# Two value blocks ahead of a weight on the queue, their shifted copies by DMA, and an attention pair moved earlier: a fused attention and MLP kernel

## The chip, the cores and the metric

The kernel runs on one core of a Trainium2 chip. The metric is the device time of one launch in microseconds (us), the median of several runs. The engines are TensorE (PE; its weight loads are shown as PEld), VectorE (DVE), ScalarE (ACT), GpSimd (POOL) and SyncE (SP). POOL and SP also issue most DMA transfers: SP's go through queue 1, ACT's through queue 10, POOL's through queue 0, and all of them run on the same 16 DMA engines.

## The reference

Attention with a sliding window of 32 positions to each side feeds a two-layer MLP with ELU:

```python
# q, k, v: (8 batches, 8 heads, 576 positions, 64), float32
scores = q @ k.T / 8
scores = where(abs(i - j) <= 32, scores, -1e9)
attn = softmax(scores)
x = (attn @ v) laid out as (4608 tokens, 512)
h = x @ w_in                               # w_in (512, 2048)
g = where(h > 0, h, exp(min(h, 0)) - 1)
out = g @ w_out                            # w_out (2048, 512), float32
```

## The kernel before

**Attention.** A batch has 9 query blocks of 64; two successive blocks make a pair, so there are 36 pairs, and pair i covers blocks 2i and 2i+1 for all heads. For a pair TensorE computes the scores (L296), ScalarE the exponential (`exponential`, L307), VectorE multiplies by a mask (`mask`, L316), TensorE multiplies by the values (`pv`, L328; a column of ones beside each head's values gives the sum), and VectorE divides (`normalize`, L337 and L340). The result is transposed, on TensorE for the first ten pairs (`x_transpose`, L349, with a copy by `x_evac`), and by a DMA after that, and lands in `xT`, the left operand of the MLP.

**Values.** A query block needs 128 values that begin 32 positions ahead of it. `V_e` holds five blocks m = 0 to 4 of 128 positions (`load_v(b, m)`, a cast from float32 to bfloat16 on POOL's queue), which serve the even query blocks. `V_o` holds the same values shifted by 64 positions, for the odd query blocks; it is made from `V_e` by moving partitions 64 to 127 to 0 to 63 and back (`rotate_v`, VectorE copies, L152). Pair 2 (query blocks 4 and 5) needs `V_e` block 2 and `V_o` block 2; pair 3 (blocks 6 and 7) needs blocks 3 of both. `V_o` block 2 is made of values 2 and 3, block 3 of values 3 and 4.

**Queries and keys.** They come in float32 by `load_qk` and are cast by `cast_qk` on ScalarE or VectorE, or come through `load_cast`, which casts on the way in on POOL's queue. TensorE transposes them (`transpose_qk`; L271 from the cast buffer, two narrow transposes for each one at L266 from `load_cast`'s). Batches 0 and 1 come in two halves, `HALF_A` and `HALF_B`.

**MLP.** 4608 tokens make 18 tiles of 256. A step is one tile and one eighth of d_ff: `mm1` (L582, 8 matmuls into `ps`), the exponential (L589), the subtraction of 1 (L591) and the max/min that makes `g_sb` (`elu`, L601), and later `mm2` (L616, 4 matmuls into `psY`). The order of the first 16 steps is: tile 0's first four, tile 1's first four, then both in turn. The weights come in quarters on POOL's queue, each serving two steps of a tile: w_in(0) and w_out(0) serve steps 0, 1, 4 and 5, w_in(1) and w_out(1) steps 2, 3, 6 and 7, quarters 2 and 3 steps 8 to 11 and 12 to 15.

**What sets the order.** It is written out by hand. The front part of the program has batch 0's first half of q and k, pairs 0 and 1 and the second half. Then a loop over steps kk runs, in this order, `elu(kk - 1)`, the tasks in slot "dve", `mm1(kk)`, the tasks in slot "mid", the second products due (`mm2`), and slot "end". `at(kk, slot, fn, ...)` puts a task there. Each engine works through its own instructions in program order, so a task that waits holds back all that stands behind it on the same engine.

The second products normally lag by two steps; for the first steps a table gives them:

```python
for n in {1: (0,), 2: (), 3: (), 4: (), 5: (2,), 6: (3, 4)}.get(
        kk, (kk - LAG,) if kk >= LAG else ()):
    mm2(n)
```

and `mm2(1)` is a task of step 2. POOL's queue is served in order. Before, after batch 0's second half of q and k, it holds w_in(0), w_out(0), values 3 and 4 of batch 0, w_in(1), w_out(1), w_in(2), w_out(2), values 0 to 2 of batch 1, w_in(3), w_out(3), values 3 and 4 of batch 1. SyncE's transfers of batch 1's and 2's q and k are held back by `gate`, a transfer of one element that reads a weight and so waits until it has landed (the first on w_out(0), the second on w_in(3)).

Of the kernel before, what the change touches and what calls it, by code (L numbers as in the profile page):

```python
# [10 lines left out]
BF16 = mybir.dt.bfloat16  # L11
# [10 lines left out]
def kernel(  # L22
# [9 lines left out]
    nc = tc.nc  # L32

    B, H, S, D = q.shape
# [3 lines left out]
    D_MODEL = H * D  # L38
# [7 lines left out]
    SJ = S // NC  # L46
    VS = 5
# [5 lines left out]
    NFO = D_FF // 128  # L53
# [7 lines left out]
    cpool = ctx.enter_context(tc.tile_pool(name="const", bufs=1))  # L61
# [32 lines left out]
    def ps_tile(shape, dt, tag, name):  # L94
# [7 lines left out]
          for i in range(2)]  # L102
    V_e = [cpool.tile([128, VS, H, VD], BF16, name=f"Ve{i}") for i in range(3)]
    V_o = [cpool.tile([128, VS - 1, H, VD], BF16, name=f"Vo{i}")
           for i in range(3)]
    w_in_sb = wpool.tile([128, NDO, D_FF], BF16, name="w_in_sb")
    w_out_sb = wpool.tile([128, NFO, D_MODEL], BF16, name="w_out_sb")
# [4 lines left out]
    WHOLE, HALF_A, HALF_B = (0, SJ), (0, SJ // 2), (1, SJ // 2)  # L112
    qk_f = {}

    def load_qk(b, which, part, engs=(nc.sync, nc.sync)):
        z, nj = part
        t = lpool.tile([128, 2, nj * D], FP32, tag=f"f{which}{nj}",
                       name=f"f{which}")
        qk_f[b, which, z] = t
        src = (q, k)[which][b, :, z * NC * nj:(z + 1) * NC * nj, :].rearrange(  # L120
            "(g h) (c j) d -> c g h (j d)", h=2, j=nj)
        for h in range(2):
            engs[h].dma_start(out=t[:, h, :], in_=src[:, :, h, :])
# [3 lines left out]

    def load_cast(b, which, part):
        z, nj = part
        t = cpool.tile([128, 2, nj * D], BF16, name=f"c{which}")  # L130
        qk_c[b, which, z] = t
        src = (q, k)[which][b, :, z * NC * nj:(z + 1) * NC * nj, :].rearrange(
            "(g h) (c j) d -> c g h (j d)", h=2, j=nj)
        for h in range(2):
            nc.gpsimd.dma_start(out=t[:, h, :], in_=src[:, :, h, :])  # L135

    def load_v(b, m):
        lo = 128 * m - WIN
        p0 = max(0, -lo)
        p1 = min(128, S - lo)  # L140
        nc.gpsimd.dma_start(  # L141
            out=V_e[b % 3][p0:p1, m, :, 0:D],
            in_=v[b, :, lo + p0:lo + p1, :].rearrange("h p d -> p h d"))
# [5 lines left out]
    def rotate_v(b, m0, m1, parts=(0, 1)):  # L149
        e, o = V_e[b % 3], V_o[b % 3]  # L150
        for z in parts:
            nc.vector.tensor_copy(o[64 * z:64 * (z + 1), m0:m1],  # L152
                                  e[64 * (1 - z):64 * (2 - z),
                                    m0 + z:m1 + z])

# [2 lines left out]
    def gate(src, dt=BF16, eng=nc.sync):  # L160
        gates[0] += 1
        t = cpool.tile([1, 1], dt, name=f"gate{gates[0]}")
        eng.dma_start(out=t, in_=src)

    def load_w_in(c):
        w = D_FF // 4
        nc.gpsimd.dma_start(
            out=w_in_sb[:, :, c * w:(c + 1) * w],
            in_=moe_w_in[:, c * w:(c + 1) * w].rearrange(
                "(o p) f -> p o f", p=128))  # L170

    def load_w_out(c):
        n = NFO // 4
        nc.gpsimd.dma_start(
            out=w_out_sb[:, c * n:(c + 1) * n, :],
            in_=moe_w_out[c * n * 128:(c + 1) * n * 128, :].rearrange(
                "(o p) f -> p o f", p=128))

    def w_in_at(c):
        return w_in_sb[0:1, 0, (c + 1) * (D_FF // 4) - 1:(c + 1) * (D_FF // 4)]  # L180
# [7 lines left out]
    def edges(i):  # L188
# [19 lines left out]
        out=masks, in_=masks, compare_op=ALU.is_ge, fill=0.0,  # L208
        base=0, pattern=[[0, 5], [-1, QB]], channel_multiplier=1)
    nc.gpsimd.affine_select(  # L210
        out=masks, in_=masks, compare_op=ALU.is_ge, fill=0.0,
# [183 lines left out]
    for which in range(2):  # L395
        load_cast(0, which, HALF_B)
    load_w_in(0)
    for mi in (0, 4):
        nc.gpsimd.affine_select(
            out=masks[:, mi, :], in_=masks[:, mi, :], compare_op=ALU.is_ge,  # L400
            fill=0.0, base=-WIN, pattern=[[0, QB]], channel_multiplier=1)
    nc.gpsimd.affine_select(
        out=masks[:, 3, :], in_=masks[:, 3, :], compare_op=ALU.is_ge,
        fill=0.0, base=128 - WIN - 1, pattern=[[0, QB]],
        channel_multiplier=-1)
    load_w_out(0)
    for m in (3, 4):
        load_v(0, m)
    for c in (1, 2):
        load_w_in(c)  # L410
        load_w_out(c)
    for m in range(3):
        load_v(1, m)
    load_w_in(3)
    load_w_out(3)
    for m in range(3, VS):
        load_v(1, m)
    gate(w_out_sb[0:1, NFO // 4 - 1, D_MODEL - 1:D_MODEL])
    for which in range(2):
        load_qk(1, which, HALF_A)  # L420
    gate(w_in_at(3))
    for which in range(2):
        load_qk(1, which, HALF_B)
    for which in range(2):
        load_qk(2, which, WHOLE)

    idle(8, "y1")
    front_cast(0, HALF_A, nc.vector)
# [6 lines left out]
    for i, tag in ((0, "s"), (1, "u")):  # L435
        scores(i, tag)
        exponential(i)
    idle(4, "y0")
    rotate_v(0, 0, 2)
    for i in (0, 1):  # L440
        mask(i)
# [10 lines left out]
    idle(2, "h1")  # L452

    tasks = {}

    def at(kk, slot, fn, *args):
        tasks.setdefault((kk, slot), []).append((fn, args))  # L460

    def run(kk, slot):
        for fn, args in tasks.get((kk, slot), ()):
            fn(*args)
# [8 lines left out]


    at(0, "mid", scores, 2, "s")
    at(0, "mid", exponential, 2)
    at(0, "mid", scores, 3, "u")
    at(1, "mid", exponential, 3)
    at(1, "dve", mask, 2)
    at(2, "dve", lambda: mm2(1))  # L480
    at(2, "dve", rotate_v, 0, 2, VS - 1)
    at(2, "dve", mask, 3)
    for i in (2, 3):
        at(2, "dve", pv, i)
        at(2, "dve", normalize, i)
        at(3, "mid" if i == 3 else "dve", x_transpose, i)
        at(3, "mid" if i == 3 else "dve", x_evac, i, nc.scalar)
    at(4, "dve", swap_pools)

    for part, kq in ((HALF_A, 7), (HALF_B, 15)):  # L490
        for which in range(2):
            at(*((kq + which, "dve") if kq == 7 else (kq - 1 + which, "mid")),
               cast_qk, 1, which, part, 0, SJ // 2,
               (nc.scalar, nc.vector)[which])
            at(kq + which, "mid", transpose_qk, 1, which, part, 0, SJ // 2,
               nc.scalar, "s")
    at(6, "dve", edges, 2)
    at(16, "dve", hold_v, 2)
    for m in range(VS):
        at(16 + m, "mid", load_v, 2, m)  # L500
    at(12, "dve", rotate_v, 1, 0, 2)
    for z in range(2):
        at(14 + z, "dve", rotate_v, 1, 2, VS - 1, (z,))
# [7 lines left out]
    for i in range(4, NPAIR):  # L511
        two = i >= FIRST_TWO
        kk, z = begin[i], i % 2 if two else 0
# [5 lines left out]
        n = kk + (3 + z if two else 2)  # L519
# [9 lines left out]
    for b in range(2, B):  # L529
# [9 lines left out]
        for n, back in enumerate((3, 2, 1, 0) if b == 2 else (10, 8, 3, 2)):  # L539
            m0 = 2 * (n // 2)  # L540
# [55 lines left out]
    def elu(kk, z=0):  # L596
        if z == 0:
            g_t[kk] = mpool.tile([128, FG, TT], BF16, tag="g_sb", name="g_sb")
        ps = psH[kk][z]
        w = ps.shape[1]  # L600
        nc.vector.scalar_tensor_tensor(  # L601
            g_t[kk][:, z * w:(z + 1) * w, :], ps, 0.0, m_t[kk][z],
            ALU.max, ALU.min)
# [3 lines left out]
    def mm2(kk):  # L607
        t, s = order[kk]
        if s == 0:
            psY[t] = [ps_tile([128, D_MODEL], FP32, g, "psY")  # L610
                      for g in (("h2", "t0") if t == 1 else ("y0", "y1"))]
        g_sb = g_t.pop(kk)
        last = t == NT - 1 and s == STEPS - 1
        for ts in range(2):
            for j in range(FG):
                nc.tensor.matmul(  # L616
                    psY[t][ts],
                    lhsT=g_sb[:, j, ts * 128:(ts + 1) * 128],
                    rhs=w_out_sb[:, s * FG + j, :],
                    start=(s == 0 and j == 0),  # L620
                    stop=(s == STEPS - 1 and j == FG - 1))
        if s == STEPS - 1:
            for ts in range(2):
                z = 1 - ts if last else ts
                eng = (nc.scalar, nc.vector)[z]
                y_sb = opool.tile([128, D_MODEL], FP32, tag=f"y_sb{z}",
                                  name="y_sb")
                copy_on(eng, y_sb, psY[t][ts])
                (nc.scalar if last and ts else nc.sync).dma_start(
                    out_t[t, :, ts, :], y_sb)  # L630

    LAG = 2
    for kk in range(NSTEP + LAG):
        run(kk, "first")
        if 1 <= kk < NSTEP:
            elu(kk - 1)
        run(kk, "dve")
        if kk < NSTEP:
            mm1(kk)
        run(kk, "mid")  # L640

        for n in {1: (0,), 2: (), 3: (), 4: (), 5: (2,), 6: (3, 4)}.get(
                kk, (kk - LAG,) if kk >= LAG else ()):
            mm2(n)
        run(kk, "end")
# [30 lines left out]
```

The softmax here doesn't subtract the row's maximum and nothing guards it: scores larger than these inputs give would overflow.

## Time and profile before

| | before |
|---|---|
| time, median of 3 runs | 311.01 us (310.62 to 311.11) |
| span of the profiled execution | 307.9 us |
| TensorE busy | 291.5 us (95%) |
| VectorE busy | 245.8 us (80%) |
| ScalarE busy | 169.4 us (55%) |
| POOL's queue 0 | 42304 packets, 9.51 MB |
| SyncE's queue 1 | 47444 packets, 35.60 MB |
| w_in from issue to landing, median of 4 | 14.0 us |
| w_out from issue to landing, median of 4 | 16.6 us |
| batch 1's halves of q and k from issue to landing, within the first 100 us | 5.4 and 7.2 us |

Times in the profile are counted from the first instruction. A line of a timeline gives start and length, the engine, the source line, what it writes and reads, how many instructions were merged, and in brackets how long the engine had been idle and who ended that. The landing of a DMA is when its last part has signalled. TensorE's busy time counts overlapping stages of its pipeline, so single groups look longer than the distance from one to the next (a first product takes 1.04 us by itself and 0.87 us in a row).

### The profile page before, as it was taken

To read this page: it belongs to the slowest core of one execution; us is meant where nothing else is said; L and a number is where in the kernel's file an instruction comes from. 1 tells how busy PE (TensorE), PEld (TensorE's weight loads), DVE (VectorE), ACT (ScalarE), POOL (GpSimd) and SP (SyncE) were. 2 spreads that over 40 slices of the span, in tenths; PEclk is the share of its full clock that TensorE was granted. 3 is DMA by queue.
4 is the path that set the end of the run, shared out by engine and by line. 5 is a ranking of instruction groups with operands and counts; after the bars stand their busy time and mean duration, and the time that the engine had idled before them with its cause. 6 is when DMAs were issued, how large, how long until landed. Compare 5 with 4: busy or idle time off the path is not lost.

```text
span 307.9 us, 7525 instructions
## 1 busy us (share of the span) xinstructions
PE 291.5 (95%) x3009; PEld 196.9 (64%) x3062; DVE 245.8 (80%) x478; ACT 169.4 (55%) x254; POOL 45.8 (15%) x64
## 2 busy tenths in 40 slices
PE   6778999999999999999999999999999999999994
PEld 2546666676666666666666666666666666666662
DVE  6776688899978788888887888888888787876663
ACT  3635656787664674767376737673636363634331
POOL 8841100952220302020202010000000000000000
PEclk9799999999999999999999999999999999999999
DMA  9999999999999899799999998377111111111011
GB/s 188 190 193 273 188 257 387 302 191 223 293 166 195 289 255 206 170 165 331 156 140 197 322 261 183 111 178 159 70 36 68 36 70 35 70 34 70 0 70 68
DMA packets 91654, 52.33 MB, mean 170 GB/s; under 512 B 76516, under 2 KB 81124, under 8 KB 91620
## 3 DMA queue, kind: packets, MB, share of 16 engines
q1 hardware_dynamic: 47444, 35.60, 47.4%
q0 software_dynamic: 42304, 9.51, 40.1%
q10 hardware_dynamic: 1872, 6.75, 5.8%
q8 instruction: 24, 0.39, 0.5%
q14 instruction: 10, 0.08, 0.1%
HBM read 36.70 MB, written 15.34 MB: 169 GB/s over the span
## 4 chain that ended last, share of the span: by engine, by line
PE 81%; DVE 7%; DMA 4%; POOL 3%; issue 2%; ACT 1%; DVEq 0%; POOLq 0%
PE ps L582 38%; PE psY L616 36%; DMA w_in_sb<-in_moe_w_in_dram 4%; PE psS L328 3%; PE psS L296 3%; DVE g_sb L601 2%; POOL Ve L141 1%; PE ptx L271 1%; DVE m_sb L591 1%; DVE x_st L340 1%; DVE pm L316 1%; ACT e_sb L589 1%; POOL c L135 1%; DVE y_sb L228 1%; PE psXT L349 1%
## 5 line engine op out<-in xcount | busy, mean ns | idle before, releaser
L589 ACT ACTIVATE e_sb<-ps 128x512 f32<-128x512 f32 (+1 forms) x145 | 86.2, 595 | 123.0 <-PE ps L582 115.4
L582 PE MATMUL ps<-xT,w_in_sb 128*128 128x256 bf16 x1152 | 149.3, 273 | 2.7 <-DVE m_sb L591 0.9
L616 PE MATMUL psY<-w_out_sb,g_sb 128*128 128x512 bf16 x525 | 139.1, 379 | 4.2 <-DMA w_out_sb<-in_moe_w_out_dram 0.9
L582 PEld LDWEIGHTS <-w_in_sb 128*128 128x128 bf16 x1152 | 110.7, 98 | 41.0 <-issue 2.3
L601 DVE SCALAR_TENSOR_TENSOR g_sb<-ps,m_sb 128x512 bf16<-128x512 f32 (+1 forms) x145 | 99.5, 686 | 13.1 <-PE ps L582 0.5
L591 DVE TENSOR_SCALAR m_sb<-e_sb 128x512 bf16<-128x512 f32 (+1 forms) x145 | 62.2, 429 | 35.3 <-ACT e_sb L589 33.3
L616 PEld LDWEIGHTS <-g_sb 128*128 128x128 bf16 x576 | 54.5, 98 | 39.9 <-DVE g_sb L601 1.6
L141 POOL DMA_DIRECT2D Ve<-in_v_dram x40 | 35.0, 885 | 130.7 <-PE psS L328 93.6
L307 ACT ACTIVATE pu<-psS 128x1024 bf16<-128x1024 f32 x36 | 36.6, 1019 | 1.9 <-PE psS L296 1.9
L340 DVE TENSOR_TENSOR x_st<-psS,rc 128x512 bf16<-128x512 f32 x36 | 24.9, 692 | 2.3 <-DMA xT<-x_st 1.1
L316 DVE TENSOR_TENSOR pm<-pu,masks 128x1024 bf16<-128x1024 bf16 x36 | 24.6, 683 | 1.4 <-ACT pu L307 1.3
L226 ACT CAST qkb<-f 128x768 bf16<-128x768 f32 (+1 forms) x30 | 25.4, 848 | 0.0
L328 PEld LDWEIGHTS <-pm 128*64 128x64 bf16 x576 | 11.2, 110 | 9.7 <-DVE pm L316 6.7
L152 DVE COPY Vo<-Ve 64x1040 bf16<-64x1040 bf16 x32 | 13.8, 431 | 1.4 <-DMA Ve<-in_v_dram 0.4
L328 PE MATMUL psS<-Ve,pm 128*64 128x65 bf16 x320 | 13.8, 196 | 0.5 <-DVE pm L316 0.3
L296 PEld LDWEIGHTS <-kT 64*128 64x128 bf16 x576 | 10.0, 97 | 5.3 <-issue 4.2
L228 DVE COPY y_sb<-psY 128x512 f32<-128x512 f32 x18 | 12.3, 686 | 1.0 <-PE psY L616 0.9
L296 PE MATMUL psS<-qT,kT 64*128 64x64 bf16 x576 | 12.4, 193 | 0.5 <-DVE kT L228 0.5
L328 PE MATMUL psS<-Vo,pm 128*64 128x65 bf16 x256 | 12.4, 196 | 0.2 <-DVE pm L316 0.2
L226 ACT COPY y_sb<-psY 128x512 f32<-128x512 f32 x18 | 10.5, 583 | 2.2 <-PE psY L616 2.2
L226 ACT COPY qT<-ptx 128x1152 bf16<-128x1152 bf16 (+2 forms) x8 | 7.5, 971 | 3.1 <-PE ptx L271 2.4
L271 PE MATMUL ptx<-ident,qkb 128*128 128x128 bf16 x90 | 7.1, 223 | 2.0 <-DVE qkb L228 1.9
(35 smaller groups left out, 68.3 us busy)
## 6 DMA issues: line engine op xcount, KB each, us to landing
out_dram<-y_sb SPq DMA_DIRECT2D x35, 256.0 KB, 2.8
f<-in_q_dram SPq DMA_DIRECT2D x12, 576.0 KB, 8.4
f<-in_k_dram SPq DMA_DIRECT2D x12, 576.0 KB, 9.2
in_dram<-qkb ACTq DMA_DIRECT2D x10, 576.0 KB, 7.3
Ve<-in_v_dram POOLq DMA_DIRECT2D x24, 128.0 KB, 10.3
w_in_sb<-in_moe_w_in_dram POOLq DMA_DIRECT2D x4, 512.0 KB, 14.0
w_out_sb<-in_moe_w_out_dram POOLq DMA_DIRECT2D x4, 512.0 KB, 16.6
Ve<-in_v_dram POOLq DMA_DIRECT2D x16, 96.0 KB, 9.5
```

The costliest lines, as they stand in the source:

```text
L141: nc.gpsimd.dma_start(out=V_e[b % 3][p0:p1, m, :, 0:D], in_=v[b, :, lo + p0:lo + p1, :].rearrange("h p d -> p h d"))
L226: nc.scalar.copy(d_, s_)
L296: nc.tensor.matmul(psS[:, h % 2, hp * 128 + z * QB:hp * 128 + (z + 1) * QB], lhsT=kT[b % 2][base:base + 64, KPAD + hp * S + QB * qb - WIN: ...
L307: nc.scalar.activation(pu, _bap(psS, [psS.ap[0], [1, 1024]]), AX.Exp, scale=SCALE)
L316: nc.vector.tensor_mul(pm, pu, _bap(mm, [mm.ap[0], [0, H], [1, 2 * QB]]))
L328: nc.tensor.matmul(psS[QB * z:QB * (z + 1), par, hp * VD:(hp + 1) * VD], lhsT=pm[:, par * HP + hp, z * QB:(z + 1) * QB], rhs=vv[:, qb // 2 ...
L340: nc.vector.tensor_mul(x_st, _bap(psS, [psS.ap[0], [VD, HP], [512, 2], [1, D]]), _bap(rc, [rc.ap[0], [2, HP], [1, 2], [0, D]]))
L582: nc.tensor.matmul(ps[:, j, :], lhsT=w_in_sb[:, do, fo * 128:(fo + 1) * 128], rhs=xT[t][:, :, do, :], start=(do == 0), stop=(do == NDO - 1))
L589: nc.scalar.activation(e_sb, ps, AX.Exp)
L591: nc.vector.tensor_scalar(m_sb, e_sb, -1.0, None, ALU.add)
L601: nc.vector.scalar_tensor_tensor(g_t[kk][:, z * w:(z + 1) * w, :], ps, 0.0, m_t[kk][z], ALU.max, ALU.min)
L616: nc.tensor.matmul(psY[t][ts], lhsT=g_sb[:, j, ts * 128:(ts + 1) * 128], rhs=w_out_sb[:, s * FG + j, :], start=(s == 0 and j == 0), stop=( ...
```

## The change

Values 3 and 4 of batch 0 go ahead of w_out(0) on POOL's queue. The shifted copies of them that `rotate_v` made on VectorE in step 2 are made by two SyncE transfers from SBUF to SBUF instead (`rotate_v_dma`). Batch 1's first half of q and k, which came in float32 through SyncE behind the first gate and was cast on ScalarE and VectorE in steps 7 and 8, comes through `load_cast` on POOL's queue, into the buffers that batch 0's second half used (the tag gives both the same buffer); the first gate goes. Pair 2's and pair 3's work stands sooner: both exponentials in step 0, both masks and both `pv` in step 1, pair 2's `normalize` and transpose in step 1, pair 3's in step 2. The second products 2 to 4 stand at steps 4 to 6, as in the rest of the program, rather than at steps 5 and 6. The purpose is to have the attention of pairs 2 and 3 out of the way before the second quarter of the weights is there, and the engines free of the casts.

```diff
     def load_cast(b, which, part):
-        t = cpool.tile([128, 2, nj * D], BF16, name=f"c{which}")
+        t = cpool.tile([128, 2, nj * D], BF16, tag=f"c{which}",
+                       name=f"c{which}")
...
+    def rotate_v_dma(b, m0, m1):
+        e, o = V_e[b % 3], V_o[b % 3]
+        for z in range(2):
+            nc.sync.dma_start(out=o[64 * z:64 * (z + 1), m0:m1],
+                              in_=e[64 * (1 - z):64 * (2 - z), m0 + z:m1 + z])
...
-    load_w_out(0)
     for m in (3, 4):
         load_v(0, m)
-    for c in (1, 2):
-        load_w_in(c)
-        load_w_out(c)
-    for m in range(3):
-        load_v(1, m)
-    load_w_in(3)
-    load_w_out(3)
-    for m in range(3, VS):
-        load_v(1, m)
-    gate(w_out_sb[0:1, NFO // 4 - 1, D_MODEL - 1:D_MODEL])
-    for which in range(2):
-        load_qk(1, which, HALF_A)
-    gate(w_in_at(3))
-    for which in range(2):
-        load_qk(1, which, HALF_B)
-    for which in range(2):
-        load_qk(2, which, WHOLE)
+    load_w_out(0)
+    load_w_in(1)
+    load_w_out(1)
...
+    for which in range(2):
+        load_cast(1, which, HALF_A)
+    load_w_in(2)
+    load_w_out(2)
+    for m in range(3):
+        load_v(1, m)
+    load_w_in(3)
+    load_w_out(3)
+    for m in range(3, VS):
+        load_v(1, m)
+    rotate_v_dma(0, 2, VS - 1)
+    gate(w_in_at(3))
+    for which in range(2):
+        load_qk(1, which, HALF_B)
+    for which in range(2):
+        load_qk(2, which, WHOLE)
...
     at(0, "mid", scores, 2, "s")
-    at(0, "mid", exponential, 2)
     at(0, "mid", scores, 3, "u")
-    at(1, "mid", exponential, 3)
-    at(1, "dve", mask, 2)
+    for i in (2, 3):
+        at(0, "mid", exponential, i)
+        at(1, "dve", mask, i)
+        at(1, "mid", pv, i)
+    at(1, "mid", normalize, 2)
+    at(1, "end", x_transpose, 2)
+    at(1, "end", x_evac, 2, nc.scalar)
     at(2, "dve", lambda: mm2(1))
-    at(2, "dve", rotate_v, 0, 2, VS - 1)
-    at(2, "dve", mask, 3)
-    for i in (2, 3):
-        at(2, "dve", pv, i)
-        at(2, "dve", normalize, i)
-        at(3, "mid" if i == 3 else "dve", x_transpose, i)
-        at(3, "mid" if i == 3 else "dve", x_evac, i, nc.scalar)
+    at(2, "dve", normalize, 3)
+    at(2, "mid", x_transpose, 3)
+    at(2, "mid", x_evac, 3, nc.scalar)
...
-            at(*((kq + which, "dve") if kq == 7 else (kq - 1 + which, "mid")),
-               cast_qk, 1, which, part, 0, SJ // 2,
-               (nc.scalar, nc.vector)[which])
+            if part is HALF_B:
+                at(kq - 1 + which, "mid", cast_qk, 1, which, part, 0, SJ // 2,
+                   (nc.scalar, nc.vector)[which])
...
-        for n in {1: (0,), 2: (), 3: (), 4: (), 5: (2,), 6: (3, 4)}.get(
+        for n in {1: (0,), 2: (), 3: ()}.get(
                 kk, (kk - LAG,) if kk >= LAG else ()):
```

## The prediction

> **What bounds the kernel now.** I read the page first, then the chain of waits in its early part, then TensorE's timeline there, then the transfers one by one.
>
> The page says that TensorE carries the kernel:
>
> ```profile
> span 307.9 us, 7525 instructions
> ...
> PE 291.5 (95%) x3009; PEld 196.9 (64%) x3062; DVE 245.8 (80%) x478; ACT 169.4 (55%) x254; POOL 45.8 (15%) x64
> ...
> PE 81%; DVE 7%; DMA 4%; POOL 3%; issue 2%; ACT 1%; DVEq 0%; POOLq 0%
> ```
>
> 81% of the chain is TensorE. The change touches only the first 40 us, so its worth is the time that TensorE loses there. The chain over those microseconds has one large piece that isn't compute:
>
> ```profile
> 11.50 11.10 DMA w_in_sb<-in_moe_w_in_dram
> 22.59 0.05 issue
> 22.64 1.06 PE ps L582 x8
> ```
>
> The second quarter of w_in, issued by POOL at 11.50, lands at 22.59, and step 2's first product starts 0.05 us later. TensorE's timeline around it (start, duration, what, and in brackets the idle time before and who ended it):
>
> ```profile
> 15.27 1.03 PE L582 MATMUL ps<-xT,w_in_sb 128*128 128x256 bf16 x8 [0.46 <-ACT xT L226]
> ...
> 16.80 1.05 PE L582 MATMUL ps<-xT,w_in_sb 128*128 128x256 bf16 x8
> 18.72 1.02 PE L616 MATMUL psY<-w_out_sb,g_sb 128*128 128x512 bf16 x3 [0.87 <-DMA w_out_sb<-in_moe_w_out_dram]
> 19.98 1.04 PE L616 MATMUL psY<-w_out_sb,g_sb 128*128 128x512 bf16 x4 [0.24 <-DVE g_sb L601]
> ...
> 22.64 1.05 PE L582 MATMUL ps<-xT,w_in_sb 128*128 128x256 bf16 x8 [0.36 <-DMA w_in_sb<-in_moe_w_in_dram]
> ...
> 25.95 1.91 PE L582 MATMUL ps<-xT,w_in_sb 128*128 128x256 bf16 x16 [0.94 <-DVE m_sb L591]
> ...
> 28.96 1.03 PE L582 MATMUL ps<-xT,w_in_sb 128*128 128x256 bf16 x8 [0.25 <-DVE g_sb L601]
> ...
> 36.62 1.04 PE L582 MATMUL ps<-xT,w_in_sb 128*128 128x256 bf16 x8
> ```
>
> Steps 0, 1, 2, 4, 6 and 9 of the MLP start there. The reader should see that the wait for w_in at 22.64 is filled: w_out and pairs 2 and 3 are done in it, and only 0.36 us is idle just before. From 15.27 to 36.62 TensorE has 21.35 us for 9 first products (0.87 each), 7 second products (0.86 each) and about 3 us of attention: 17 us of work, so about 4.4 us of gaps. From 36.62 to 60 the stage view has 22.64 busy of 23.38: what is won or lost before step 9 is carried to the end.
>
> SyncE's timeline, and the DMA view from there to the first packets, show how a SyncE transfer fares beside a full POOL queue:
>
> ```profile
> 18.69 0.76 SPq L163 DMA_DIRECT2D gate<-w_out_sb  x1
> 19.51 1.22 SPq L123 DMA_DIRECT2D f<-in_q_dram  x2
> ```
>
> ```profile
> q0 software_dynamic: 1037, 0.96, 126.2%
> q1 hardware_dynamic: 2, 0.00, 0.1%
> ```
>
> The last two lines (queue, packets, MB, share) are of the window 18.69 to 23.37. In these 4.7 us queue 1 (SyncE) moved two tiny packets, those of the gate, while POOL's queue moved 1037. The first q load, issued at 19.51, moved nothing until 23.37 and landed 5.8 us after issue; the second, issued at 20.12, took 7.9.
>
> [...] The trace agrees that the queues share (after 23.37 they move 184 and 194 packets in 2 us), but shows a long delay before a newcomer's turn: up to 22.70 queue 1 moved nothing and queue 0 896 packets, 56 per engine. [...] the window 4.10 to 7.52 had TensorE busy 1.86 us and the next ran at clock 0.50; the window 17.76 to 21.17 had 2.25 us busy and the clock stayed.
>
> **The change, part by part.**
>
> *Order on POOL's queue.* The queue is served in order, and V3 and V4 move from behind w_out(0) to behind w_in(0). POOL can issue all of them by 13 us as before. w_in(0) landed at 15.06; V3 came 1.47 after its predecessor (18.68 to 20.15) and V4 0.36 later. So V3 lands near 16.5 and V4 near 16.9 instead of 20.15 and 20.51; w_out(0), taking 3.6, near 20.5 instead of 18.68; w_in(1) has the same bytes ahead of it as before and lands at 22.6, plus up to 0.6 for the copies below. The wait that bounded the stage isn't shortened.
>
> *The shifted copies.* Two VectorE copies of 0.44 us (0.88 at 20.17) go. Two SyncE transfers of 64 rows by 2,080 bytes (133 KB) take their place, issued when V3 and V4 have landed, about 16.5 and 17.1 (an issue takes 0.6). No transfer of this shape is in the trace. Bounds: 3.2 us from issue to landing, the median of the transposing x_st transfers later in the run, mostly beside a quiet POOL queue, would give 20.1; the 7.9 us of the second q load would give 25. I take 5.8 us, the first q load's: 288 KB, about as much as both copies together, and issued into the same full queue (w_out(0), w_in(1), w_out(1) and the casts queued ahead). Nothing on SyncE is harmed, since only the gate on w_in(3), due at 38, stands behind. So the copies are there at 16.9 + 5.8 = 22.7.
>
> *Who waits for them.* The products pv of pairs 2 and 3 stand in step 1, ahead of second product 0, and TensorE takes them in order. Each needs an odd block from the shifted copy. Behind them wait second product 0 (its w_out is there at 20.5), pair 2's transpose, second product 1, and step 2. On VectorE normalize 2 waits for pv and elu(1) stands behind it. TensorE is done with step 1 at about 17.7 and idles until 22.7: 5 us where there were about 1.8. After it: two pv (0.38 each), second product 0 (0.86), a transpose (0.22), second product 1 (0.86): 2.7 us, step 2 starts at 25.4 against 22.64. In the gap a clock window has well under 1.86 us of work, so I add a spell of half clock. If the windows fall as before, it covers 21.17 to 24.58: 1.9 us at half speed lose about 0.9; half of this overlaps VectorE's own wait there, so 0.5. Step 2 starts at 25.9.
>
> *From step 2 to step 9.* Step 4 needs elu(2): from 22.64 to the end of g_sb at 25.58 the trace has 2.95 us. Then five first products (4.35), five second (4.30), the two q and k transposes (0.55 and 0.6, eighteen narrow ones each, priced by the same form at 11.83 and 13.57): 9.8. Second products 2 to 6 now stand in their places, w_out(1) being there at about 26. The casts of q (ACT, 1.14) and k (DVE, 0.75) are gone, and with them the wait of 0.41 before the k transposes at 35.24. Sum 12.7, against 22.64 to 36.62 = 14.0 before: the rearrangement saves 1.3.
>
> *Batch 1's first half on POOL's queue.* Four transfers of 0.7 us each (10.28, 11.05, 11.74, 12.47 were their like) stand before w_in(2); four loads of equal read bytes leave SyncE, which had shared the engines from 23.4 to 31. The same bytes in other order: w_in(2) near 31 (30.89 before, needed at about 35), w_in(3) near 39 (needed after 44). They reuse the buffers of batch 0's second half, whose transposes end at 14.2; POOL waits there for about 1 us, with w_out(0), w_in(1) and w_out(1) already queued. Nothing.
>
> *Sum.* Step 9 starts at 25.9 + 12.7 = 38.6 against 36.62: 2.0 us later. 311.0 + 2.0 = 313.0.
>
> **The rivals.**
>
> *The copies land by 20.1*, in 3.2 us. For it: they come from SBUF and are small. Against: the two tiny gate packets waited 4.0 us too. Then pv runs ahead of w_out(0), step 2 starts when w_in(1) lands, about 22.8, step 9 at 22.8 + 12.7 = 35.5, 1.1 us sooner: 309.9. Chance 0.20.
>
> *The copies cost what the reordering brings.* They land near 21.2 (4.3 us, less than any load beside the full queue took): step 2 at 23.9, step 9 at 36.6: 311.0. Chance 0.13.
>
> *A longer wait or a longer slow clock.* Landing at 24, or a second window of 3.4 us at half clock: 1.3 to 1.7 more, 314.5. [...] Chance 0.12.
>
> **How the numbers follow.** The forecast has 0.55 and gives 313.0. The range 310.0 to 314.6 runs from just over the first rival to the last, since a landing time between 20 and 24 is the one large unknown, and each microsecond of it past 20.1 moves the end by one. Slower is the forecast and the last rival, 0.67; same 0.13; faster 0.20.
>
> **What would show it.** Right: TensorE's timeline has a gap of 4 us or more after step 1, ended by pv waiting for the Vo copies; V3 lands by 17, the copies after 21.5; the clock falls to 0.5 for a window near 22; step 2 starts after 25, and from there to step 9 takes under 13.2. Wrong: the copies land within 3.5 us; or V3 and V4 land no earlier than 18; or the first products from step 2 on wait for w_out(1), w_in(2) or the cast halves.

## The result and the profile after

| | before | after |
|---|---|---|
| time, median (4 runs each) | 311.06 us (310.62 to 312.13) | 314.0 us (313.68 to 314.37) |
| ratio, 95% interval | | 1.009 (1.0061 to 1.0119) |
| span of the profiled execution | 307.9 us | 312.5 us |

In this comparison the change makes the kernel slower by 2.9 us; 2.0 were forecast. Beside the experiments it cost more, 4.5 us (1.0146): the changed kernel took 314.5 us there, the kernel before only 309.7. The profiled execution of before is of that kind: it took 309.6 us, less than any of the four timed ones here, so the two spans lie 4.6 us apart. Three lines of the page of the changed kernel, to be set beside those of before:

```profile
span 312.5 us, 7554 instructions
...
PE 294.4 (94%) x3027; PEld 198.3 (63%) x3080; DVE 244.2 (78%) x475; ACT 168.3 (54%) x253; POOL 48.2 (15%) x68
...
L336 PE MATMUL psS<-Vo,pm 128*64 128x65 bf16 x256 | 12.5, 199 | 3.7 <-DMA Vo<-Ve 3.4
```

VectorE and ScalarE have lost their copies and casts (245.8 to 244.2 and 169.4 to 168.3 us), and the span grew all the same. The third line is new: TensorE waits 3.4 us for the shifted copy. TensorE's timeline of the changed kernel has it in place:

```profile
16.16 1.03 PE L593 MATMUL ps<-xT,w_in_sb 128*128 128x256 bf16 x8 [0.46 <-ACT xT L234]
...
17.70 1.05 PE L593 MATMUL ps<-xT,w_in_sb 128*128 128x256 bf16 x8
19.74 0.22 PE L336 MATMUL psS<-Ve,pm 128*64 128x65 bf16 x1 [1.00 <-DVE pm L324]
23.39 0.22 PE L336 MATMUL psS<-Vo,pm 128*64 128x65 bf16 x1 [3.43 <-DMA Vo<-Ve]
...
27.60 1.04 PE L593 MATMUL ps<-xT,w_in_sb 128*128 128x256 bf16 x8
...
30.58 1.05 PE L593 MATMUL ps<-xT,w_in_sb 128*128 128x256 bf16 x8 [0.85 <-DVE g_sb L612]
...
40.74 1.04 PE L593 MATMUL ps<-xT,w_in_sb 128*128 128x256 bf16 x8
```

Steps 0, 1, 2, 4 and 9 start at 16.16, 17.70, 27.60, 30.58 and 40.74. In step 1, behind first product 1, one matmul of pv runs at 19.74; the next needs V_o and stands until 23.39, and second product 0 with it, although its w_out had landed at 20.0. The stage view of the changed kernel (busy time of the engines, then the granted clock, DMA share and GB/s) shows what this does to the clock:

```profile
17.76:23.39 5.63, 1.20 (x12) 0.74 (x11) 2.74 (x5) 2.39 (x4) 1.54 (x3) 1.00 1.22 226
23.39:27.60 4.21, 3.99 (x42) 2.20 (x44) 2.30 (x5) 0.58 (x1) 2.28 (x3) 0.59 1.22 205
27.60:40.74 13.14, 12.08 (x116) 8.48 (x117) 8.26 (x17) 6.54 (x10) 3.42 (x5) 1.00 1.60 190
```

TensorE is busy 1.20 of 5.63 us; when work comes back it runs at clock 0.59 on average, and work that takes 2.98 us at full clock (shown under e6) takes 4.21. The two copies themselves, by SyncE's timeline and the landing times of the Vo tile:

```profile
17.06 1.22 SPq L161 DMA_DIRECT2D Vo<-Ve  x2
```

```profile
DMA to landing us min/median/max: 5.4/5.6/5.7
```

Step 0 starts 0.9 us later than before (16.16 against 15.27), on work that the change doesn't touch. Up to about 13 us its matmuls took as long as those at half clock: the 32 score matmuls at 9.44 took 1.04 us, as in the profile of before at clock 0.50 (9.03), against 0.64 us at full clock in e1. The clock column shows 1.00 there, but the clock records of this execution begin only at 13.6 us, so this is read from the durations alone. Single executions also wait 2 to 3 us for a late transposing DMA now and then (TensorE 2.0 us in the profile of e9, VectorE 3.0 us in that of e11). So the experiments are read by two measures: the ratio of times, and in the profile the distances between the starts of step 0, step 2 and step 9.

| profile of | step 0 to 2 | step 2 to 9 | sum | ratio to before (95% interval) |
|---|---|---|---|---|
| before | 7.37 | 13.98 | 21.35 | 1 |
| changed, first comparison | 11.44 | 13.14 | 24.58 | 1.009 (1.0061 to 1.0119) |
| changed, with the experiments (e8) | 12.91 | 13.53 | 26.44 | 1.0146 (1.0122 to 1.017) |
| e1 copies on VectorE | 8.23 | 13.13 | 21.36 | 1.0026 (1.0008 to 1.0044) |
| e2 second products first | 8.98 | 13.49 | 22.47 | 1.0045 (1.0023 to 1.0068) |
| e3 half by cast alone | 7.08 | 13.81 | 20.89 | 1.0024 (1.0008 to 1.0039) |
| e4 gap filled, 18 | 12.65 | 13.28 | 25.93 | 1.010 (1.0061 to 1.0138) |
| e5 short backlog | 9.96 | 13.44 | 23.40 | 1.0055 (1.0036 to 1.0074) |
| e6 gap filled, 26 | 11.12 | 13.31 | 24.43 | 1.011 (1.0078 to 1.0142) |
| e7 interleaved | 7.36 | 13.33 | 20.69 | 1.0006 (0.9989 to 1.0022) |
| e9 values first alone | 7.09 | 13.91 | 21.00 | 1.0002 (0.9974 to 1.003) |
| e10 copies by DMA alone | 12.57 | 14.81 | 27.38 | 1.0206 (1.0172 to 1.024) |
| e11 copies split | 7.55 | 13.14 | 20.69 | 0.9972 (0.9955 to 0.9989) |

The kernel before took 309.7 to 309.8 us beside the experiments. The ratios leave out one execution each of e2, e3, e5 and e11 that ran over 1.5% above the kernel's fastest, and they are not exactly the ratios of the medians given below.

### The profile page after: what moved, and what is told of

The parts are those of the page before. It is cut to its first block, busy times and chain, and to the rows that moved or that the text cites. A ratio compares the mean times of both kernels' runs of the same rounds, so it can differ in the third digit from the quotient of the medians.

```text
span 312.5 us, 7554 instructions
## 1 busy us (share of the span) xinstructions
PE 294.4 (94%) x3027; PEld 198.3 (63%) x3080; DVE 244.2 (78%) x475; ACT 168.3 (54%) x253; POOL 48.2 (15%) x68
## 4 chain that ended last, share of the span: by engine, by line
PE 66%; DMA 18%; POOL 5%; DVE 4%; SPq 3%; issue 2%; ACT 1%; DVEq 0%; POOLq 0%
PE ps L593 31%; PE psY L627 30%; DMA Ve<-in_v_dram 6%; DMA w_out_sb<-in_moe_w_out_dram 4%; DMA w_in_sb<-in_moe_w_in_dram 4%; POOL Ve L142 3%; DMA f<-in_k_dram 3%; PE psS L336 3%; PE psS L304 2%; SPq L123 2%; DMA xT<-x_st 1%; DVE g_sb L612 1%; POOL c L136 1%; DVE x_st L348 1%; DVE m_sb L602 1%
## 5 line engine op out<-in xcount | busy, mean ns | idle before, releaser
L234 ACT CAST qkb<-f 128x768 bf16<-128x768 f32 (+1 forms) x29 | 24.3, 838 | 0.0
L153 DVE COPY Vo<-Ve 64x1040 bf16<-64x1040 bf16 x30 | 12.8, 427 | 1.1 <-DMA Ve<-in_v_dram 0.2
L234 ACT COPY xT<-psXT 128x512 bf16<-128x512 bf16 x10 | 5.9, 587 | 8.1 <-PE psXT L357 8.0
L345 DVE RECIPROCAL rc<-psS 128x8 f32<-128x8 f32 x36 | 7.1, 198 | 3.6 <-PE psS L336 3.6
```

The lines of the kernel that those rows point to most:

```text
L234: nc.scalar.copy(d_, s_)
```

## The experiments

Theory: the wait for the two SyncE copies, with the half clock behind it, is the whole loss. Rivals: the new order on POOL's queue is the loss; or the latency is one that any SyncE transfer has there.

### e1: the copies back on VectorE

```diff
-    rotate_v_dma(0, 2, VS - 1)
...
+    at(1, "dve", rotate_v, 0, 2, VS - 1)
     for i in (2, 3):
         at(0, "mid", exponential, i)
         at(1, "dve", mask, i)
```

> The changed kernel with the shifted copies of values 3 and 4 back on VectorE, in step 1 ahead of the masks. Theory (the wait for the two SyncE copies, and the half clock that it brings, are the loss): pv of pair 2 starts near 20.5 us instead of 23.4, no clock window drops near 24, step 2 starts when w_in(1) is there, near 23.5 instead of 27.6, and the time falls by 3.5 to 4.5 us, to about 310, a little under the kernel before. Rival (the new order on POOL's queue is the loss, through w_out(0) and w_in(1) landing later): the time stays within 1 us of the changed kernel's 314.0.

Measured: 310.69 us, 1.0026 (1.0008 to 1.0044), step 2 at 23.44. TensorE's timeline of this kernel:

```profile
19.92 0.22 PE L336 MATMUL psS<-Ve,pm 128*64 128x65 bf16 x1 [2.12 <-DVE pm L324]
...
20.91 1.04 PE L627 MATMUL psY<-w_out_sb,g_sb 128*128 128x512 bf16 x4
...
22.57 1.04 PE L627 MATMUL psY<-w_out_sb,g_sb 128*128 128x512 bf16 x4 [0.20 <-DVE g_sb L612]
```

Most of the loss goes when the copies go back to VectorE (1.0026 instead of 1.0146, about 3.7 us of the 4.5), and the queue's new order stays: the first rival falls. The 0.8 us that are left are about what the cast half costs alone (e3). It isn't under the kernel before, though, as had been expected. From 16.92 to 23.35 VectorE is busy 6.15 of 6.43 us, and elu(1), which second product 1 at 22.57 needs, stands behind the copies, both masks and normalize 2. So step 2 comes 1.1 us after w_in(1) has landed (22.3), and the 0.85 us that are saved between steps 2 and 9 only make that good.

### e2: the DMA copies kept, second products 0 and 1 ahead of pv

```diff
-        at(1, "mid", pv, i)
-    at(1, "mid", normalize, 2)
-    at(1, "end", x_transpose, 2)
-    at(1, "end", x_evac, 2, nc.scalar)
     at(2, "dve", lambda: mm2(1))
-    at(2, "dve", normalize, 3)
-    at(2, "mid", x_transpose, 3)
-    at(2, "mid", x_evac, 3, nc.scalar)
+    for i in (2, 3):
+        at(2, "dve", pv, i)
+        at(2, "dve", normalize, i)
+        at(2, "mid", x_transpose, i)
+        at(2, "mid", x_evac, i, nc.scalar)
```

> The changed kernel, copies still by SyncE, but pv, normalize and the transposes of pairs 2 and 3 stand in step 2 behind second products 0 and 1. Theory (the copies' latency hurts because TensorE's order puts other work behind them): second product 0 starts near 20 us when w_out(0) lands, the copies still land near 23.3, step 2 starts near 24.3, the clock stays at 1.0, and the time falls by about 3 us, to about 311. Rival (the latency itself is the cost, whatever stands behind it): step 2 still starts after 26 and the time stays above 313.

Measured: 311.75 us, 1.0045 (1.0023 to 1.0068). The copies landed at 22.4 and 23.1, as late as in the changed kernel, and step 2 started at 24.23. TensorE's timeline has the second products ahead of pv:

```profile
20.40 2.88 PE L625 MATMUL psY<-w_out_sb,g_sb 128*128 128x512 bf16 x8 [2.56 <-DMA w_out_sb<-in_moe_w_out_dram]
23.20 0.26 PE L336 MATMUL psS<-Ve,pm 128*64 128x65 bf16 x1
```

With the same latency, the order decides over some 3 us (1.0045 against 1.0146 for the changed kernel beside the experiments). It is TensorE's order and with it VectorE's: elu(1) no longer stands behind normalize 2. A half-clock window at 21.1 remained in the profiled execution, where none was expected: TensorE had waited 2.56 us for w_out(0) too, which leaves 1.60 us of work in 18 to 22, where e1 had 1.90 and kept clock 1.00. That this difference decides the clock isn't shown.

### e3: batch 1's first half by cast, alone on the kernel before

The casts stand where the change has them; w_in(2) and what follows it on POOL's queue move down with them.

```diff
-    gate(w_out_sb[0:1, NFO // 4 - 1, D_MODEL - 1:D_MODEL])
-    for which in range(2):
-        load_qk(1, which, HALF_A)
...
+    for which in range(2):
+        load_cast(1, which, HALF_A)
+    load_w_in(2)
+    load_w_out(2)
```

> The kernel before with one part of the change alone: batch 1's first half of q and k by load_cast on POOL's queue ahead of w_in(2), without the first gate and without the casts on ScalarE and VectorE. Theory: the same bytes in another order, w_in(2) lands near 31 and w_in(3) near 38.5 as before; the wait of about 0.4 us for the k cast in step 8 goes, and w_out(1) no longer shares with SyncE's loads: 310.4 us, 0.3 to 0.8 less than before. Rival (the casts ahead of w_in(2) delay the weights): w_in(2) lands after 33, first product 8 waits, 1 us more than before.

Measured: 310.31 us, 1.0024 (1.0008 to 1.0039). The profile agrees with the theory up to step 9 (w_in(2) at 30.7, w_in(3) at 38.4, 0.46 us less from step 0 to 9), the time doesn't: instead of a gain of 0.3 to 0.8 us there is a small loss, 0.24%. (The 310.31 us lie near the expected 310.4 only because the kernel before took 309.76 us here.) The rival, late weights, isn't seen either. Of the 0.46 us, 0.32 were left at the last first product of the profiled execution. Why the time isn't lower stays open.

### e4 and e6: the gap filled with matmuls on zeros

```diff
+    at(1, "mid", idle, 18, "y1")      # e6: 26
     for i in (2, 3):
         at(0, "mid", exponential, i)
```

> The changed kernel with 18 matmuls on zeros (about 3.9 us at full clock) in TensorE's gap, behind first product 1 and ahead of pv of pair 2; they compute nothing that is used. Theory: the copies still land near 23.3, but the clock doesn't fall to 0.5 after the gap; from the copies' landing to step 2 takes 2.8 us instead of 4.3, and the time falls by about 1.5 us, to about 312.5. Rival (the half clock is hidden behind VectorE's chain from pv to elu(1)): within 0.5 us of 314.0.

> The changed kernel with 26 matmuls on zeros (5.6 us at full clock) in the gap instead of 18, so that TensorE is busy until the copies land. In the run with 18 the gap from 21.8 to 23.9 was left, the profiled execution still had a half-clock window at 24.8 and took 312.2, while executions of it with a mean clock of 0.997 or more took 310.1 to 310.3. Theory: no execution has the half-clock window after the gap, the mean clock is 0.997 or more unless the start is slow, and the median is 1.5 to 2 us under the changed kernel's on the same chip. Rival: the filler itself delays pv, or the half clock was hidden: within 0.5 us of it.

With 18, 312.42 us. The filler ended at 21.8, and the profiled execution still had a half-clock window, at 24.8. The spread of the single executions is more telling: those with a mean clock of 0.997 or more had spans of 310.1 to 310.3, the others 311.1 to 314.2. With 26, five of six executions had a mean clock of 0.997 or more and spans of 310.5 to 311.6, against 312.1 to 312.9 for the five of the changed kernel beside them. TensorE's timeline and the stage view of the profiled execution with 26:

```profile
17.50 5.77 PE L395 MATMUL ps_idle<-zeros 128*128 128x512 bf16 x26
...
23.20 0.22 PE L336 MATMUL psS<-Ve,pm 128*64 128x65 bf16 x1
...
26.18 1.04 PE L594 MATMUL ps<-xT,w_in_sb 128*128 128x256 bf16 x8
```

```profile
22.50:26.18 3.68, 3.48 (x48) 1.69 (x47) 2.30 (x5) 0.58 (x1) 1.23 (x2) 1.00 1.23 206
```

From the start of pv at 23.20 to step 2 at 26.18 it takes 2.98 us at full clock. The changed kernel took 4.21 us in its first profile (23.39 to 27.60, at half clock from 23.85 to 27.27) and 4.84 in its second, where pv started at 23.35 and step 2 at 28.19, all at half clock:

```profile
23.50:28.19 4.69, 4.69 (x44) 2.42 (x42) 2.30 (x5) 0.58 (x1) 2.78 (x4) 0.50 1.21 204
```

So the half clock costs 1.2 to 1.9 us there. The filler takes some of that back: the copies had landed at 22.5, and pv stood behind it until 23.20. By the medians of the times (312.97 against 314.47) filling the gap gains 1.5 us. The intervals of the two ratios overlap a little (1.0078 to 1.0142 and 1.0122 to 1.017), so this size is less sure than the one in the profiles.

### e5: the copies issued into a short queue

```diff
     load_w_out(0)
+    gate(V_e[0][0:1, 4, 0, 0:1], eng=nc.gpsimd)
     load_w_in(1)
     load_w_out(1)
```

> The changed kernel with a one-element transfer on POOL's queue ahead of w_in(1) that waits for V4, so that when SyncE issues the two copies (17.1 and 17.7) POOL's queue holds w_out(0) alone and not w_in(1), w_out(1) and the casts. Theory (a newcomer waits for the descriptors already queued on the engines): the copies' first packets move near 18.5 to 19 instead of 20.9 and they land by 21.5 instead of 22.5 and 23.3; w_in(1) lands about 1 us later, near 24.2, and then sets step 2; the time falls by 1.5 to 3 us. Rival (a SyncE transfer beside a busy POOL queue takes some 5.5 us whatever is queued): first packets at 20.9 and landings at 22.5 to 23.3 as before.

Measured: 311.81 us, 1.0055 (1.0036 to 1.0074). POOL's and SyncE's timelines, and the landing times of the Vo tile, in this kernel:

```profile
18.44 0.54 POOL L171 DMA_DIRECT2D gate<-Ve  x1 [6.97 <-DMA Ve<-in_v_dram]
18.97 0.77 POOL L175 DMA_DIRECT2D w_in_sb<-in_moe_w_in_dram  x1
```

```profile
17.83 1.18 SPq L161 DMA_DIRECT2D Vo<-Ve  x2
```

```profile
DMA to landing us min/median/max: 2.6/2.7/2.8
```

The same two transfers take 2.7 us instead of 5.6. In the changed kernel queue 0 moved 786 packets, on average 49 for each of 16 engines, between the issue at 17.06 and the first packet of the copies at 20.90:

```profile
DMA packets 786, 0.78 MB, mean 203 GB/s; under 512 B 25, under 2 KB 786, under 8 KB 786
```

Here it moved 99, 6 per engine, up to 19.03. The fixed 5.5 us of the rival is ruled out, and a newcomer that waits for what already stands on the engines fits both kernels. The landings came even sooner than expected (20.7 and 21.0). The price is that the weights behind come 1.4 us (w_in(1)) to 2.8 us (w_in(2)) later. Nor does the half clock go away: TensorE still waited 1.00 us for the mask and 1.99 us for the copies, and the clock was 0.50 from 22.05 to 25.46. Step 2 started at 25.23, behind second product 1 and not, as expected, when w_in(1) landed (24.6).

### e7 and e11: tries for a version ahead of both

```diff
-    rotate_v_dma(0, 2, VS - 1)
...
-    for i in (2, 3):
-        at(0, "mid", exponential, i)
-        at(1, "dve", mask, i)
-        at(1, "mid", pv, i)
-    at(1, "mid", normalize, 2)
-    at(1, "end", x_transpose, 2)
-    at(1, "end", x_evac, 2, nc.scalar)
-    at(2, "dve", lambda: mm2(1))
-    at(2, "dve", normalize, 3)
-    at(2, "mid", x_transpose, 3)
-    at(2, "mid", x_evac, 3, nc.scalar)
+    at(0, "mid", exponential, 2)
+    at(1, "dve", rotate_v, 0, 2, VS - 1)      # e11: part 0 alone
+    at(1, "dve", mask, 2)
+    at(1, "mid", idle, 8, "y1")
+    at(1, "mid", lambda: nc.scalar.copy(      # e11 alone
+        V_o[0][64:128, 2:VS - 1], V_e[0][0:64, 3:VS]))
+    at(1, "mid", exponential, 3)
+    at(1, "end", pv, 2)
+    at(2, "dve", mask, 3)
+    at(2, "dve", lambda: mm2(1))
+    at(2, "dve", pv, 3)
+    for i in (2, 3):
+        at(2, "dve", normalize, i)
+        at(2, "mid", x_transpose, i)
+        at(2, "mid", x_evac, i, nc.scalar)
```

The diff is that of e7; the comments tell what e11 has in its place or besides.

> A try for a version ahead of both: the changed kernel's queue and casts, the copies on VectorE in step 1, and TensorE's order second product 0, pv of pair 2, second product 1, pv of pair 3, step 2, with elu(1) ahead of both normalizations, exponential 3 behind step 1's exponential, and 8 matmuls on zeros behind first product 1 to keep the clock. Theory: step 2 starts when w_in(1) lands, near 22.4 instead of 23.4 with the copies on VectorE alone, no half clock near 21; step 9 starts near 35.6, 1 us ahead of the kernel before; about 1 us (0.3%) under it. Rival (what is won before step 9 is given back at a later wait, as in the run with the cast half alone, whose step 9 was 0.27 us earlier and whose end was not): within 0.2% of the kernel before.

> The interleaved version (which in its profile was bound by VectorE, busy without a break from 17.6 to 24.4) with the second of the two copies on ScalarE behind step 1's exponential. Theory: VectorE loses 0.44 us there, step 2 starts 0.4 us sooner after step 0 than in that version (7.4 us), and the time is 0.2 to 0.4 us under it: 0.998 to 1.000 of the kernel before. Rival (ScalarE delays exponential 3, mask 3 and pv of pair 3 by its 1 us copy): step 2 no sooner, the time the same or more.

Interleaved: 310.0 us, 1.0006 (0.9989 to 1.0022), no difference. VectorE's timeline, in the part that should have been shorter:

```profile
18.18 0.69 DVE L613 SCALAR_TENSOR_TENSOR g_sb<-ps,m_sb 128x512 bf16<-128x512 f32 x1
18.90 0.88 DVE L153 COPY Vo<-Ve 64x1040 bf16<-64x1040 bf16 x2
19.82 0.69 DVE L324 TENSOR_TENSOR pm<-pu,masks 128x1024 bf16<-128x1024 bf16 x1
20.43 0.67 DVE L603 TENSOR_SCALAR m_sb<-e_sb 128x512 bf16<-128x512 f32 x1
21.20 0.69 DVE L613 SCALAR_TENSOR_TENSOR g_sb<-ps,m_sb 128x512 bf16<-128x512 f32 x1
21.81 0.68 DVE L324 TENSOR_TENSOR pm<-pu,masks 128x1024 bf16<-128x1024 bf16 x1
```

It has no gap: with the values early, VectorE is what bounds step 1. TensorE's second product 1 waited for its g_sb, pv of pair 3 followed it, and step 2 (23.30) again comes after w_in(1) (22.4):

```profile
21.95 1.04 PE L628 MATMUL psY<-w_out_sb,g_sb 128*128 128x512 bf16 x4 [0.46 <-DVE g_sb L613]
...
23.30 1.05 PE L594 MATMUL ps<-xT,w_in_sb 128*128 128x256 bf16 x8
```

With one of the two copies on ScalarE: 309.15 us, 0.9972 (0.9955 to 0.9989), the only version under the kernel before, by 0.28%. Its profile can't show the expected cause. The profiled execution took 312.7 us, far above the median, and step 2 started 7.55 us after step 0 instead of 7.36: w_out(0) landed only at 20.8 there (19.8 in the interleaved one), TensorE waited 0.56 us for it, and what stands behind it followed almost without a gap. So the gain is measured; where it comes from isn't shown.

### e9 and e10: one part alone on the kernel before

The values first (e9):

```diff
-    load_w_out(0)
     for m in (3, 4):
         load_v(0, m)
+    load_w_out(0)
```

The copies by DMA (e10; it has `rotate_v_dma` as the changed kernel has it):

```diff
+    rotate_v_dma(0, 2, VS - 1)
     gate(w_out_sb[0:1, NFO // 4 - 1, D_MODEL - 1:D_MODEL])
...
-    at(2, "dve", rotate_v, 0, 2, VS - 1)
```

> The kernel before with one part alone: values 3 and 4 ahead of w_out(0) on POOL's queue; everything else as before. Theory: V3 and V4 land near 16.5 and 17.2, w_out(0) near 20.2 instead of 18.7, w_in(1) at 22.4 as before; second product 0 waits for w_out(0), and second product 1, pv of pairs 2 and 3 follow it, so step 2 starts near 23.2 instead of 22.6: 0.3 to 0.7 us more than before, since TensorE's old order has nothing to do with the early values. Rival (early values alone win): 0.3 us or more less than before.

> The kernel before with one part alone: the shifted copies of values 3 and 4 by two SyncE transfers ahead of the first gate, instead of on VectorE. V3 and V4 land at 20.2 and 20.5 there, behind them w_in(1), w_out(1), w_in(2) and w_out(2) are queued. Theory: the copies land 5.3 us after issue, near 25.5 to 26, pv of pairs 2 and 3 wait for them and hold back step 2, which starts near 26.7 instead of 22.6; a half-clock window falls behind the gap: 4 to 5.5 us more than before. Rival (copies off VectorE are free or a gain of their 0.88 us): within 1 us of the kernel before.

The values first alone: 1.0002 (0.9974 to 1.003). The loss of 0.3 us or more that I expected isn't seen: w_out(0) landed at 19.4, w_in(1) at 22.0 and step 2 started at 22.32. The interval reaches from 0.8 us less to 0.9 us more, so it excludes neither that loss nor a gain of the same size; it does exclude that the order on POOL's queue by itself is the change's loss. The DMA copies alone: 316.66 us, 1.0206 (1.0172 to 1.024), 6.4 us more where 4 to 5.5 were expected, and more than the whole change costs. TensorE's timeline:

```profile
19.97 1.04 PE L622 MATMUL psY<-w_out_sb,g_sb 128*128 128x512 bf16 x4 [0.19 <-DVE g_sb L607]
26.77 0.26 PE L334 MATMUL psS<-Vo,pm 128*64 128x65 bf16 x1 [5.62 <-DMA Vo<-Ve]
```

The copies were issued at 20.62 and 21.21 and took 5.4 and 5.5 us; in the changed kernel the earlier values hide 3.4 us of that (a landing at 23.3 instead of 26.7).

The remaining run is the changed kernel itself beside the others:

> The changed kernel itself, beside the others on one chip. Theory: 1.009 times the kernel before as in the first comparison, about 2.8 us more; every run has a mean clock under 0.995[...]. Rival (the half clock depends on where the windows fall): some runs have a mean clock of 0.998 or more and are about 2 us shorter.

Measured: 314.47 us, 1.0146 (1.0122 to 1.017); every execution had a mean clock of 0.995 or less, nearly as the theory wanted, the profiled one with half clock from 22.2 to 29.0. The cost is larger than the theory's 2.8 us. The changed kernel took nearly the same in both comparisons (314.0 and 314.5), the kernel before didn't (311.06 and 309.71), so the two ratios lie outside each other's intervals. What made the kernel before slower in the first comparison is open. The window of half clock in its profile, between 7.52 and 10.93, doesn't explain it, since that execution took 309.6 us.

## Why the prediction was right

The path was forecast rightly: the copies take the time of a SyncE transfer beside a full queue, pv waits for them, and everything up to step 2 waits behind pv. The size was not. Step 0 to step 9 was forecast to take 23.3 us instead of 21.35, 2.0 more; the two profiles show 24.58 and 26.44, 3.2 and 5.1 more. That the forecast 2.0 us came near the measured 2.9 is in part luck: the kernel before took 311.06 us in the first comparison and 309.7 in every later one. Beside the experiments the change cost 4.5 us, over twice the forecast.

**Queue.** V3 and V4 were forecast for 16.5 and 16.9 and landed at 17.0 and 17.6; w_out(0) for 20.5, landed 20.0; w_in(1) for 22.6 to 23.2, landed 23.2: the order in which POOL issued them, as it was before (w_out(0) 18.7, V3 and V4 20.2 and 20.5, w_in(1) 22.6). The wait for w_in(1) wasn't shortened, and e9 shows no effect of the order alone within 0.9 us.

**Copies.** Landing forecast 22.7, measured 22.5 and 23.3, as 5.4 and 5.7 us after issue against the 5.8 taken from the first q load. Choosing the nearest transfer into the same full queue, over the 3.2 us of a quieter one, decided the prediction; e5 shows that the short latency exists too (2.7 us), with little queued.

**The queue behind the wait.** That second product 0, elu(1) and step 2 stand behind pv was the step that turned a late transfer into lost time; e2 confirms it, with step 2 at 24.23 and the copies as late as ever.

**The term that was mis-sized** is the half clock. From pv to step 2 I summed 2.7 us of work and 0.5 us for the clock. The work was right (2.98 us at full clock in e6); the clock cost 1.2 and 1.9 us in the two profiles. That half clock would follow the gap was an estimate from the one spell in the early part of the profile before: the 3.42 us ahead of it had TensorE busy for 1.86. In the first profile of the changed kernel the 3.41 us ahead of the spell had 0.45 us busy; 1.94 us busy in 17.02 to 20.43 were followed by clock 1.00. Two assumptions failed. I placed the window by counting on in steps of 3.41 us from the spell in the profile before, at 21.17 to 24.58, so that only 1.9 us of it held work; it lay at 23.85 to 27.27 in the first profile, all of it behind the gap, and the second profile had half clock for twice as long, from 22.2 to 29.0. And I took half of the loss to overlap VectorE's own wait, but in the first profile TensorE was busy 3.99 of the 4.21 us: elu(1) was done at 25.41, before second product 1 could start at 26.21. VectorE's and TensorE's timelines:

```profile
24.73 0.68 DVE L612 SCALAR_TENSOR_TENSOR g_sb<-ps,m_sb 128x512 bf16<-128x512 f32 x1
```

```profile
26.21 1.55 PE L627 MATMUL psY<-w_out_sb,g_sb 128*128 128x512 bf16 x4
```

**Step 2 to step 9.** Forecast 12.7, measured 13.14 (13.53 in the second profile, whose half clock reaches into it): the rearrangement saves 0.84 instead of 1.3. The cast half was priced at nothing apart from the wait for the k cast; alone it lost 0.24% (e3), for a reason that stays open.

The rival in which the copies land within 3.2 us and the change wins 1.1 us was half right about its trigger: e5 has them in 2.7 us. But the shorter queue that this takes lets the weights come later, the clock still falls, and the time stays 1.0055 of before.

## What to carry to other kernels

Before moving a copy from a compute engine to a DMA, look up what is queued on the DMA engines at the moment of issue: 133 KB took 2.7 us with 6 packets per engine ahead of the first of its own and 5.6 us with 49. If an instruction that waits must stay on a busy engine, put behind it only what can't run without it; here moving two second products ahead of it was worth some 3 us with the transfer as late as before. And count an idle gap on TensorE twice, once for its length and once for the half clock that can follow it (here 1.2 to 1.9 us behind a gap of over 4 us).

## What the runs showed of the hardware that was not expected

The time from issue to the first packet of the first copy was nearly constant over five kernels with a full POOL queue (the changed one, e2, e4, e6 and e10): 3.8 to 3.9 us, while 49 to 50 packets of queue 0 per engine went ahead, whatever the issue time (16.5 to 17.1, and 20.6 us). That the queue is full is not enough to foretell it. In the kernel before the second gate, issued at 38.37, had its first packet at 40.04, after 1.67 us, though queue 0 was as busy and 58 of its packets per engine went ahead; they were smaller, 0.30 MB for 930 packets against 0.82 MB for the 896 ahead of the first gate, which waited 4.0 us.

The same kernel falls into the half clock in some executions and not in others where the gap is short. With 18 fillers about 2 us of the gap were left, and three executions of six had a mean clock of 0.997 or more; their spans were 310.1 to 310.3 us, the others' 311.1 to 314.2. That the clock is the only difference between them isn't shown.
